# A planned attention and GELU kernel: all engines' order found anew, pair 0's values in one transfer per four heads, the last output tile in two halves

## The chip, the cores and the metric

The kernel runs on one core of a Trainium2 chip. The metric is device microseconds (us) of one execution. Before the change the median of three runs is 739.65 us (738.93 to 741.37).

## The reference, cut to what matters

Batch 8, 8 heads, 576 rows of 64 in q, k and v, and 32 packed queries p per head; then a feed-forward layer from 512 through 2048 to 512 on 4608 tokens. Everything is float32.

```python
def sm_attn(qq, kk, vv):
    s = scale * np.matmul(qq, kk.transpose(0, 1, 3, 2))
    s = s - np.max(s, axis=-1, keepdims=True)
    a = np.exp(s)
    a = a / (np.sum(a, axis=-1, keepdims=True) + 1e-09)
    return np.matmul(a, vv)
p_packed = sm_attn(p, k, v)          # 32 packed rows per head
out = sm_attn(q, p_packed, p_packed)
x = out.transpose(0, 2, 1, 3).reshape(4608, 512)
h = x @ w_in                         # 512 -> 2048
g = 0.5 * h * (1.0 + erf(h * inv_sqrt2))
return g @ w_out                     # 2048 -> 512
```

## The kernel before, in words

**What is computed where.** The eight batches form four pairs. Heads are taken in chunks of four: chunk 1_0 in a name is batch 1, first four heads. For a chunk TensorE (PE) turns k and q by transposes (`turn`, L461: tiles km, qm, copied to kT, qT on ScalarE (ACT) or VectorE (DVE)), multiplies the packed queries with kT (s1, L538), and DVE and ACT make the first softmax of it. Its exponentials are turned (e1Tm, e1Tn, L650) and multiplied with the values v (tile pp, L680), turned back (ppTm, L695) and copied to the SBUF tile pp. The second scores (s2, L538) are qT times pp; their softmax, on DVE and ACT with one chunk of pair 0 partly on GpSimd (POOL), gives the weights a2 (plain) and a2T (a pair of rounded parts, L804 and L806).

Instead of attention times w_in, the kernel multiplies pp with w_in first (wps, L1017, copied to wp) and then wp with the weights (h, L1083; L1074 for batch 0's first column block, where the plain weights serve). GELU follows on ACT (graw, L1106), its result is split into a rounded part and a rest (g, L1113 on ACT and L1115 on DVE), and these go against w_out (o, L1136 to L1138, three products for float32). Sums over column blocks lie in acc (L1200).

**Units and steps.** d_ff is cut into 4 blocks of 512 columns; a unit is one pair with one block, so 16 units of 8 steps (2 batches by 4 column tiles of 128), 128 steps in all. Step n has a hidden product h_n and output products o. The rows that a batch of 576 leaves over from tiles of 128 are gathered in t4 and multiplied after each unit (o_edge); the last of these ends the program. Units 0 to 3 also decode w_in and w_out (`decode`, L946 and L942 load, then ACT, DVE and POOL) and store them in DRAM (`keep`, L998) for the later units.

**What sets the order.** Nothing is ordered by hand. While the program is built, a small planner (`Order`, with `Op` for each piece of work) plays the engines through with costs that stand in the code, and the order in which it issues pieces becomes each engine's fixed instruction order. Of the ready pieces it takes the one with the lowest step number. The tables FIRST (pair 0 and unit 0), SECOND (pair 1) and LATER (pairs 2, 3) hold these step numbers; LEAD, PATIENCE and STEADY move weights and set how far a fitting piece may be taken ahead. A transfer's planned length comes from its cost: number of pieces and bytes over DMA_RATE, where the byte count is a fitted one, not the real one.

All transfers are issued by SyncE (SP) in one queue in planned order. A buffer that is not free stops this queue: of x raw tiles (k and q) there are 3, of raw values 1 (chunk 0_1 uses a buffer of wp instead), of raw weights 3.

Until the first output product, the planner fills PE's free time with products of a constant tile (`keep_warm`, L1056, tile still). They stand in PE's instruction order like others.

**Lines that the change touches.** `load` (k and q), `load_values` (v; pair 0 uses `sixths`, 96 partitions with six rows of each of four heads, in two pieces of 256 and 128 values per head and partition), `held`, `weight` and `decode`, `edge_output`, and the tables.

Of the kernel before, what the change touches and what calls it, by code (L numbers as in the profile page):

```python
# [42 lines left out]
DMA_FIRST, DMA_ISSUE, DMA_START, DMA_END, DMA_RATE = 2.0, 0.5, 0.6, 0.9, 390e3  # L43

DMA_DEPTH = 8
DMA_SLACK, DMA_EARLY = 2.0, 50.0
TABLE_SWITCH = 1.3
PE_START, PE_WINDOW, PE_LEAST = 1.0, 3.41, {True: 0.45, False: 0.9}
IDLE, IDLE_END = 0.11, 150.0
# [2 lines left out]


LATER = {
    "p": (11.96, 4.31),
    "k": (9.37, 6.72, -0.79, 5.76),
    "v": (4.46, 5.97, 10.35, 23.09),
    "q": (7.94, 14.96, 23.74, 28.45),
    "scores1": (-2.56, 15.38),
    "softmax1": (8.43, -1.96, 4.16, 5.99),  # L60
    "packed": (-50.68, -7.0, 15.26, 19.97),
    "scores2": (22.79, 15.93),
    "softmax2": (-77.33, -62.89, 23.22, 15.85),
    "weights2": (32.15, -50.98, -6.98, 38.51),
    "groups1": ((0, 1, 2, 3),),
    "groups2": ((0, 1), (2, 3)),
}

SECOND = {
    "p": (20.75, 3.34),  # L70
    "k": (7.37, -42.06, 10.92, 22.21),
    "v": (8.64, 9.54, 12.08, 14.62),
    "q": (24.0, -36.23, 19.77, 24.5),
    "scores1": (-7.96, 8.69),
    "softmax1": (23.58, 28.48, 10.35, 11.22),
    "packed": (13.43, 9.46, -19.64, 17.8),
    "scores2": (-42.32, 23.44),
    "softmax2": (3.08, -54.42, 7.07, 36.08),
    "weights2": (7.31, 23.91, -34.4, 27.85),
    "groups1": ((0,), (1,), (2,), (3,)),  # L80
    "groups2": ((0,), (1,), (2,), (3,)),
}

AHEAD = 12
LEAD = {"load": 41.5, "decode": -5.8, "packed_w_in": 12.3}

PATIENCE = {PE: -50.7, ACT: -58.2, DVE: 28.6, POOL: 30.2, DMA: -16.5}
STEADY = {PE: 50.0, ACT: -44.9, DVE: 8.1, POOL: -12.5, DMA: 13.9}

FIRST = {  # L90
    "p": (-317.54, -182.89),
    "k": (-327.51, -303.62, -196.02, -185.2),
    "v": (-249.99, -74.38, -178.71, -155.31),
    "q": (-216.51, -212.03, -93.83, -161.52),
    "w": (-194.95, -219.42, -192.91, -163.65, -152.43, -145.84, -71.43, -169.98),
    "scores1": (-221.37, -193.05, -72.18, -73.16),
    "softmax1": (-51.37, 6.81, -347.66, -175.1),
    "packed": (-180.43, -262.75, -182.09, 5.22),
    "scores2": (-233.03, -212.25, -155.17, -251.0),
    "softmax2": (-146.14, -327.21, -189.22, -190.15),  # L100
    "weights2": (-183.99, -138.74, -180.16, -74.68),
    "decode": (-178.03, -74.98, -180.05, -168.82, -193.1, -214.82, -193.35, 17.95),
    "packed_w_in": (-192.13, -218.39, -190.45, -146.14),
    "weights_split": (-94.13, -184.63, -65.79, -335.34),
    "groups1": ((0, 1), (2, 3)),
    "groups2": ((0,), (1,), (2,), (3,)),
    "gpsimd": (0,),
    "copy": ("ACT", "DVE", "DVE", "DVE"),
    "banks": (False, True, True, True),
    "turn": {"k": ("ACT", "DVE", "ACT", "ACT"), "q": ("ACT", "DVE", "ACT", "ACT")},  # L110
}


# [39 lines left out]
class Op:  # L153
# [1 line left out]


    def __init__(self, engine, cost, step, fn, takes=(), table=None, busy=True, port=False, tiled=False):
        self.engine, self.cost, self.step, self.fn = engine, cost, step, fn
        self.takes, self.table, self.busy, self.tiled = takes, table, busy, tiled

        self.port = (engine == POOL and cost > 0) or port


class Order:
# [147 lines left out]
def packed_attention_gelu_ffn(ctx: ExitStack, tc: tile.TileContext, q, k, v, p, w_in, w_out, out):  # L312
# [108 lines left out]
    def load(bt, name, src, c, step):  # L421

        def rows(t):
            nc.sync.dma_start(t, src[bt.b, 4 * c:4 * c + 4].rearrange("h (x s) d -> (h x) (s d)", s=2 * NT))

        def blocks(t):

            t = t.rearrange("p (n a) -> p n a", a=32)
            for hh in range(2):
                h0 = 4 * hh + 2 * c  # L430
                view = src[bt.b, h0:h0 + 2].rearrange("g (c b) (j a) -> j b (g c) a", b=32, j=2)
                for j in range(2):
                    i = 2 * hh + j
                    nc.sync.dma_start(t[32 * i:32 * i + 32], view[j])

        cost, fn = ((1, 570e3), rows) if bt.b < 2 else ((4, 1800e3, 1.1), blocks)
        bt.raw[name, c] = yield Op(DMA, cost, step, fn, [(xraws, f"{name}_{bt.n}_{c}")])
        fire(bt.loaded[name, c])

# [34 lines left out]
    def sixths_of(t):  # L474

        if len(t.shape) > 2:
            t = t.rearrange("p a b c -> p (a b c)").bitcast(F32)
        return t[:96, 0:24 * D].rearrange("p (g t d) -> p g t d", g=4, t=6)

    def load_values(s, step):  # L480
        heads = slice(4 * s.hh, 4 * s.hh + 4)

        def sixths(t):
            src = v[s.b, heads].rearrange("g (p t) d -> p g t d", t=6)
            for part in (slice(0, 4), slice(4, 6)):
                nc.sync.dma_start(
                    sixths_of(t)[:, :, part].rearrange("p g t d -> p g (t d)"),
                    src[:, :, part].rearrange("p g t d -> p g (t d)"))

        def fn(t):  # L490
            main, tail = values_of(t)
            nc.sync.dma_start(
                main.rearrange("p g t d -> p g (t d)"), v[s.b, heads, 0:512].rearrange("g (p t) d -> p g (t d)", t=4))
            nc.sync.dma_start(tail, v[s.b, heads, 512:S].rearrange("g p d -> p g d"))

        cost, fn = ((2, 700e3), sixths) if s.b < 2 else ((2, 900e3, 0.6), fn)
        s.v = yield Op(DMA, cost, step, fn, [(s.v_ring, f"v_{s.n}")])
        fire(s.v_loaded)

# [315 lines left out]
    reached = [Event() for _ in range(NU * 8)]  # L815

    def held(task, step):
        if step >= 1:
            yield reached[min(int(step), NU * 8 - 1)]
        yield from task  # L820
# [90 lines left out]
    def weight(u, i, load_steps, steps):  # L911


        ring_, home, k = (wis, wi, i) if i < 2 else (wos, wo, i - 2)
        n, f = f"{u}_{i}", u % NF
        if u >= NF:
            yield stored[f, i]
            home[u, k] = yield Op(
                DMA, (1, 524e3), steps[0],
                lambda t: nc.sync.dma_start(t.bitcast(F32), scratch[f, i]), [(ring_, f"w_{n}")])  # L920
            for part in range(parts_of(i)):
                fire(w_ready[u, i, part])
            return
        yield [decode(u, i, part, *at) for part, at in enumerate(zip(load_steps, steps))]
        d = scratch[f, i] = dram.tile([P, 2, FB], F32, name=f"ws_{f}_{i}")
        start(keep(f, i, d, home[u, k], steps[-1] + 4))

    def decode(u, i, part, load_step, step):
        n, f = f"{u}_{i}_{part}", u % NF
# [15 lines left out]
            src = w_in[2 * P * i:2 * P * i + 2 * P, c0:c0 + FB // 2].rearrange("(g p) n -> p g n", g=2)  # L945
            nc.sync.dma_start(t.rearrange("p (g n) -> p g n", g=2), src.bitcast(I32))  # L946

        raw = yield Op(DMA, (1, 540e3 if i < 2 else 500e3), load_step, fetch, [(raws, f"wraw_{n}")])
        low, high = words(raw)[:, :, 0], words(raw)[:, :, 1]

        def both_words(both):
# [14 lines left out]
            port=True)  # L966
        raws.give(raw)
        if i < 2:
            if (u, i) not in wi:
                got = yield from one(wis, f"w_{u}_{i}", POOL, step)  # L970
                wi[u, i] = got
            d, cols = wi[u, i], slice(part * (FB // 2), (part + 1) * (FB // 2))

            def halves(x):
                return x.rearrange("p (g n) -> p g n", g=2)

            yield Op(
                POOL, 1.25, step,
                lambda: nc.gpsimd.tensor_tensor(d[:, :, cols].bitcast(I32), halves(t), halves(full), ALU.add))  # L979
        else:  # L980
            def split():
# [306 lines left out]
```

## Time and profile before

| | us |
|---|---|
| median of 3 runs | 739.65 |
| profiled execution | 740.66 |
| its span (first to last instruction) | 738.9 |
| PE busy | 728.0 |
| DVE busy | 399.6 |
| ACT busy | 357.4 |
| POOL busy | 149.5 |

The profiled execution is 1.8 us longer than its span and 1.0 us above the median. PE busy counts the products of the constant tile too. Times in the trace are from the span's start. In the trace, a product that fills a PSUM tile first used by constant products carries that tile's name, so "PE idle L680" is a packed-values product; only "idle L1056" is the constant tile.

### The profile page before, as it was taken

To read this page: it belongs to the slowest core of one execution; us is meant where nothing else is said; L and a number is where in the kernel's file an instruction comes from. 1 tells how busy PE (TensorE), PEld (TensorE's weight loads), DVE (VectorE), ACT (ScalarE), POOL (GpSimd) and SP (SyncE) were. 2 spreads that over 40 slices of the span, in tenths; PEclk is the share of its full clock that TensorE was granted. 3 is DMA by queue.
4 is the path that set the end of the run, shared out by engine and by line. 5 is a ranking of instruction groups with operands and counts; after the bars stand their busy time and mean duration, and the time that the engine had idled before them with its cause. 6 is when DMAs were issued, how large, how long until landed. Compare 5 with 4: busy or idle time off the path is not lost.

```text
span 738.9 us, 13425 instructions
## 1 busy us (share of the span) xinstructions
PE 728.0 (99%) x5395; PEld 592.4 (80%) x5395; DVE 399.6 (54%) x604; ACT 357.4 (48%) x600; POOL 149.5 (20%) x328
## 2 busy tenths in 40 slices
PE   7999999999999999999999999999999999999998
PEld 5767888787877888788787888787877888888886
DVE  2779687888778432533756632553565821333332
ACT  2668674666766543454434444453443643323221
POOL 1334564654401101001100101100011110111010
PEclk8999999999999999999999999999999999999999
DMA  9967597667965697441734959263345703021022
GB/s 269 320 211 150 181 244 209 209 201 193 244 169 107 209 124 182 62 147 61 148 97 136 273 77 166 65 147 109 82 126 118 243 14 123 37 82 61 5 94 88
DMA packets 156589, 106.77 MB, mean 145 GB/s; under 512 B 123248, under 2 KB 132464, under 8 KB 156528
## 3 DMA queue, kind: packets, MB, share of 16 engines
q1 hardware_dynamic: 156528, 105.93, 55.3%
q8 instruction: 42, 0.69, 0.4%
q14 instruction: 19, 0.16, 0.1%
HBM read 83.89 MB, written 22.02 MB: 143 GB/s over the span
## 4 chain that ended last, share of the span: by engine, by line
PE 95%; DMA 3%; SPq 1%; issue 1%; DVE 0%; ACT 0%
PE h L1083 26%; PE o L1136 17%; PE o L1138 16%; PE o L1137 16%; PE wps L1017 4%; PE s L538 2%; PE o_edge L1136 2%; PE o_edge L1138 2%; PE o_edge L1137 2%; PE idle L1056 2%; DMA k<-in_k_dram 2%; DMA wraw<-in_moe_w_out_dram 2%; PE pp L680 2%; PE e1Tm L639 1%; PE h L1074 1%
## 5 line engine op out<-in xcount | busy, mean ns | idle before, releaser
L1083 PEld LDWEIGHTS h<-a2T,wp 128*128 128x128 f32 x1488 | 209.6, 188 | 11.4 <-ACT graw L1106 1.0
L1083 PE MATMUL h<-a2T,wp 128*128 128x288 f32 x1488 | 216.4, 294 | 0.8 <-ACT graw L1106 0.8
L1115 DVE TENSOR_TENSOR g<-graw,g 128x512 fp32r<-128x512 f32 x128 | 93.7, 734 | 212.4 <-ACT g L1113 212.2
L1106 ACT ACTIVATE graw<-h 128x576 f32<-128x576 f32 x127 | 82.8, 652 | 257.2 <-PE h L1083 197.0
L1136 PE MATMUL o<-w,g 128*128 128x512 f32 x508 | 205.7, 405 | 0.0
L1138 PE MATMUL o<-w,g 128*128 128x512 f32 x508 | 199.2, 392 | 0.0
L1137 PE MATMUL o<-w,g 128*128 128x512 f32 x508 | 198.8, 391 | 0.0
L1126 POOL CAST t<-graw 128x64 fp32r<-128x64 f32 x128 | 35.6, 278 | 504.1 <-ACT graw L1106 343.2
L1136 PEld LDWEIGHTS o<-w,g 128*128 128x128 f32 x508 | 95.3, 188 | 38.3 <-issue 22.5
L1138 PEld LDWEIGHTS o<-w,g 128*128 128x128 f32 x508 | 95.3, 188 | 21.9
L1137 PEld LDWEIGHTS o<-w,g 128*128 128x128 f32 x508 | 95.5, 188 | 14.8
L1200 DVE TENSOR_TENSOR acc<-o,acc 128x512 f32<-128x512 f32 x96 | 64.0, 686 | 41.6 <-PE o L1138 41.5
L1113 ACT CAST g<-graw 128x512 fp32r<-128x512 f32 x128 | 79.3, 620 | 9.9 <-PE o L1138 6.9
L1127 POOL TENSOR_TENSOR t<-graw,t 128x64 fp32r<-128x64 f32 x128 | 45.6, 356 | 10.2
L1033 DVE TENSOR_TENSOR wp<-wps,wp 128x1024 fp32r<-128x1024 f32 (+1 forms) x32 | 37.7, 1186 | 18.0 <-ACT wp L1028 17.9
L1028 ACT CAST wp<-wps 128x1024 fp32r<-128x1024 f32 x30 | 30.1, 1014 | 22.4 <-PE wps L1017 22.4
L1017 PE MATMUL wps<-w,pp 64*32 64x512 f32 (+1 forms) x544 | 34.4, 574 | 0.0
L1056 PE MATMUL idle<-still 128*128 128x256 bf16 x231 | 31.8, 288 | 1.1 <-DVE still L394 1.1
L1056 PEld LDWEIGHTS <-still 128*128 128x128 bf16 x231 | 22.8, 102 | 9.1 <-issue 4.5
L952 ACT ACTIVATE wt<-wraw 128x512 f32<-128x512 f32 x32 | 21.6, 676 | 16.3 <-POOL w L993 7.5
L979 POOL TENSOR_TENSOR w<-wt 128x512 int32<-128x512 int32 x16 | 22.0, 1373 | 28.2 <-DVE mx L610 15.9
L960 DVE TENSOR_SCALAR wt<-wt 128x512 int32<-128x512 int32 x32 | 25.4, 792 | 1.1
(127 smaller groups left out, 663.4 us busy)
## 6 DMA issues: line engine op xcount, KB each, us to landing
w<-ws SPq DMA_DIRECT2D x72, 512.0 KB, 4.9
ws<-w SPq DMA_DIRECT2D x24, 512.0 KB, 4.8
wraw<-in_moe_w_in_dram SPq DMA_DIRECT2D x16, 512.0 KB, 5.3
wraw<-in_moe_w_out_dram SPq DMA_DIRECT2D x16, 512.0 KB, 3.6
k<-in_k_dram SPq DMA_DIRECT2D x48, 144.0 KB, 4.7
q<-in_q_dram SPq DMA_DIRECT2D x48, 144.0 KB, 4.8
out_dram<-acc SPq DMA_DIRECT2D x27, 256.0 KB, 2.3
v<-in_v_dram SPq DMA_DIRECT2D x12, 512.0 KB, 5.6
```

The lines of the kernel that those rows point to most:

```text
L1017: nc.tensor.matmul(t[r0:r0 + 32, hh, :m], lhsT=pp[b][rows, hh, r0:r0 + 32], rhs=wi[u, hh][rows, g, cols], start=True, stop=True)
L1033: yield Op(DVE, 0.16 + 1.04 * m / FB, step, lambda: nc.vector.tensor_tensor(lo, x, hi.bitcast(F32), ALU.subtract))
L1056: nc.tensor.matmul(bank(t)[:, :256], lhsT=still[:, :P], rhs=still, start=True, stop=True)
L1083: nc.tensor.matmul(t[:, half, :HALF], lhsT=w[:, wpart, ch, fc], rhs=a2T[b, ch][:, apart, half * HALF:(half + 1) * HALF], start=ch == 0 and ...
L1106: lambda raw: nc.scalar.activation(raw.rearrange("p (a n) -> p a n", a=2), t[:, :, :HALF], AF.Gelu),
L1113: g = yield Op(ACT, 0.52, lead, lambda g: nc.scalar.copy(g[:, 0], main), [(gts, f"g_{n}")])
L1115: DVE, 0.6, lead, lambda: nc.vector.tensor_tensor(g[:, 1], main, g[:, 0].bitcast(F32), ALU.subtract),
L1127: nc.gpsimd.tensor_tensor(dst[:, 1], side, dst[:, 0].bitcast(F32), ALU.subtract)
L1136: nc.tensor.matmul(t, lhsT=g[0], rhs=w[:, 0], start=first, stop=False)
L1137: nc.tensor.matmul(t, lhsT=g[0], rhs=w[:, 1], start=False, stop=False)
L1138: nc.tensor.matmul(t, lhsT=g[1], rhs=w[:, 0], start=False, stop=last)
L1200: yield Op(DVE, 0.6, n, lambda: nc.vector.tensor_tensor(a, x, a, ALU.add))
```

## The change

Four things change.

1. The numbers in FIRST, SECOND, LATER, LEAD, PATIENCE and STEADY, with a new table `keep` for the stores of decoded weights. Chunk 0_1 takes GpSimd's part instead of chunk 0_0.
2. The planner's lengths of the first transfers: k and q of pair 0 from 570e3 to 620e3 bytes, w_in from 540e3 to 590e3, w_out from 500e3 to 530e3, values of pair 0 from two pieces of 700e3 together to one of 1000e3; the 2 us that it adds to a landing now start at 6 us instead of 50 us.
3. The values of pair 0 come in one transfer per chunk, with 384 values per head and partition.
4. The last o_edge (unit 15) is made in two halves of 256 columns, each with its own addition and store.

```diff
-DMA_SLACK, DMA_EARLY = 2.0, 50.0
+DMA_SLACK, DMA_EARLY = 2.0, 6.0
...
-    "v": (-249.99, -74.38, -178.71, -155.31),
...
+    "v": (-334.59, -165.81, -182.85, -96.68),
...
-        cost, fn = ((1, 570e3), rows) if bt.b < 2 else ((4, 1800e3, 1.1), blocks)
+        cost, fn = ((1, 620e3), rows) if bt.b < 2 else ((4, 1800e3, 1.1), blocks)
...
         def sixths(t):
-            src = v[s.b, heads].rearrange("g (p t) d -> p g t d", t=6)
-            for part in (slice(0, 4), slice(4, 6)):
-                nc.sync.dma_start(
-                    sixths_of(t)[:, :, part].rearrange("p g t d -> p g (t d)"),
-                    src[:, :, part].rearrange("p g t d -> p g (t d)"))
+            nc.sync.dma_start(
+                sixths_of(t).rearrange("p g t d -> p g (t d)"), v[s.b, heads].rearrange("g (p t) d -> p g (t d)", t=6))
...
-        cost, fn = ((2, 700e3), sixths) if s.b < 2 else ((2, 900e3, 0.6), fn)
+        cost, fn = ((1, 1000e3), sixths) if s.b < 2 else ((2, 900e3, 0.6), fn)
...
-        raw = yield Op(DMA, (1, 540e3 if i < 2 else 500e3), load_step, fetch, [(raws, f"wraw_{n}")])
+        raw = yield Op(DMA, (1, 590e3 if i < 2 else 530e3), load_step, fetch, [(raws, f"wraw_{n}")])
...
+        if u == NU - 1:
+            yield from last_output(u, n)
+            return
...
+    def last_output(u, n):
+        a, r0, m = acc[NP - 1, 4], (NP - 1) * 2 * S + 4 * P, DM // 2
+        def add(t, cols):
+            yield Op(DVE, 0.36, n, lambda: nc.vector.tensor_tensor(a[:, cols], t[:, 0, :m], a[:, cols], ALU.add))
+            yield Op(DMA, (1, 131e3), n, lambda: nc.sync.dma_start(out[r0:r0 + P, cols], a[:, cols]))
+        for k in range(2):
+            cols = slice(k * m, k * m + m)
+            def product(t, cols=cols):
+                for c in range(NC4):
+                    g = t4[u, c]
+                    three(t[:, 0, :m], (g[:, 0], g[:, 1]), wo[u, c][:, :, cols], c == 0, c == NC4 - 1)
+            t = yield Op(PE, 1.38, n, product, [(wide, f"o_{u}_edge_{k}")])
+            start(add(t, cols))
```

How the instructions move shows at three places. The names end in running numbers; the numbers before them are batch and chunk (v_0_1 is chunk 0_1) or, for w and wraw, unit, tile and part (tiles 0 and 1 are w_in, 2 to 5 w_out).

SP's queue, its first two dozen rows. Before:

```order
L424 DMA k_0_1_93<-in_k_dram 128x1152
L486 DMA v_0_0_97<-in_v_dram 96x4x256
L486 DMA v_0_0_97<-in_v_dram 96x4x128
L946 DMA wraw_0_0_1_104<-in_moe_w_in_dram 128x2x512
L424 DMA q_0_0_109<-in_q_dram 128x1152
...
L424 DMA k_1_1_257<-in_k_dram 128x1152
L486 DMA v_0_1_275<-in_v_dram 96x4x256
L486 DMA v_0_1_275<-in_v_dram 96x4x128
L998 DMA ws_0_0_318<-w_0_0_78 128x1024
...
L424 DMA q_1_0_416<-in_q_dram 128x1152
L998 DMA ws_0_1_415<-w_0_1_79 128x1024
L486 DMA v_1_0_554<-in_v_dram 96x4x256
```

The same stretch with the change:

```order
L425 DMA k_0_0_97<-in_k_dram 128x1152
L485 DMA v_0_0_101<-in_v_dram 96x4x384
L425 DMA q_0_0_105<-in_q_dram 128x1152
...
L485 DMA v_0_1_123<-in_v_dram 96x4x384
...
L425 DMA k_1_1_281<-in_k_dram 128x1152
L941 DMA wraw_0_5_0_316<-in_moe_w_out_dram 128x1024
L997 DMA ws_0_0_379<-w_0_0_78 128x1024
L485 DMA v_1_0_419<-in_v_dram 96x4x384
L941 DMA wraw_0_4_0_430<-in_moe_w_out_dram 128x1024
...
L425 DMA q_1_0_559<-in_q_dram 128x1152
```

Values of chunk 0_1 stood behind all of k and are now the ninth row; values of chunk 1_0 stood behind all of q and now stand ahead of batch 1's q.

PE, around the packed values of batch 0. Before:

```order
L461 MATMUL km_1_1_2_425<-ident_71,k_1_1_257 128x128 x3
L538 MATMUL idle_349<-kT_1_0_357,pT_1_307 32x288 x8
L680 MATMUL pp_0_1_440<-v_0_1_275,e1T_0_1_309 32x64 x24
...
L538 MATMUL s1_1_1_493<-kT_1_1_405,pT_1_307 32x288 x8
...
L680 MATMUL idle_505<-v_0_0_97,e1T_0_0_474 32x64 x24
L538 MATMUL s2_0_1_0_544<-qT_0_1_333,pp_0_502 32x288 x4
...
L1017 MATMUL wps_0_0_1_601<-w_0_0_78,pp_0_502 32x256 x2
```

With the change:

```order
L678 MATMUL idle_310<-v_0_1_123,e1T_0_1_229 32x64 x24
...
L678 MATMUL idle_367<-v_0_0_101,e1T_0_0_354 32x64 x24
...
L508 MATMUL pTm_1_432<-ident_71,p_1_147 128x128 x2
L693 MATMUL ppTm_0_1_435<-ident_71,pn_0_1_416 128x128
...
L693 MATMUL idle_439<-ident_71,pn_0_0_437 128x128
...
L1016 MATMUL idle_259<-w_0_0_78,pp_0_446 32x256 x2
...
L536 MATMUL s2_0_0_0_479<-qT_0_0_238,pp_0_446 32x288 x4
...
L462 MATMUL km_1_0_0_490<-ident_71,k_1_0_232 128x128 x3
```

Batch 0's packed values, its first wps and its first second scores stood behind batch 1's k and its first scores; now they stand ahead of them.

PE, the first output products. Before:

```order
L1017 MATMUL wps_0_1_1_879<-w_0_0_78,pp_1_734 32x256 x2
...
L1074 MATMUL h_2_977<-a2_0_716,wp_0_0_84 128x288 x4
L1136 MATMUL idle_868<-w_0_2_537,g_0_891 128x512
...
L1074 MATMUL h_3_1022<-a2_0_716,wp_0_0_84 128x288 x4
L1083 MATMUL h_4_1035<-a2T_1_0_971,wp_0_1_478 128x288 x6
L1083 MATMUL h_4_1035<-a2T_1_1_1020,wp_0_1_478 128x288 x6
```

With the change:

```order
L1073 MATMUL h_2_908<-a2_0_746,wp_0_0_84 128x288 x4
L536 MATMUL s2_1_1_929<-qT_1_1_705,pp_1_736 32x288 x8
L1135 MATMUL idle_893<-w_0_2_426,g_0_913 128x512
...
L1016 MATMUL wps_0_1_1_953<-w_0_0_78,pp_1_736 32x256 x2
...
L1073 MATMUL h_3_983<-a2_0_746,wp_0_0_84 128x288 x4
...
L1016 MATMUL wps_0_1_0_1022<-w_0_0_78,pp_1_736 32x256 x2
...
L1082 MATMUL h_4_1060<-a2T_1_0_920,wp_0_1_361 128x288 x6
L1082 MATMUL h_4_1060<-a2T_1_1_1044,wp_0_1_361 128x288 x6
```

Two wps products of batch 1 moved behind the first output product, and the outputs of steps 0 to 2, not of step 0 alone, now stand ahead of h_4. Ahead of the first output product PE's order has 231 constant products before and 208 with the change; otherwise the same pieces but for those two wps.

## Rows read from the trace of the kernel before

**Rows 1.** The page: busy time and share of PE; its granted clock by slices.

```profile
PE 728.0 (99%) x5395; PEld 592.4 (80%) x5395; DVE 399.6 (54%) x604; ACT 357.4 (48%) x600; POOL 149.5 (20%) x328
...
PEclk8999999999999999999999999999999999999999
```

**Rows 2.** Waits of PE: engine, line, releaser: us in total, times, longest.

```profile
PE km L461 <- DMA k<-in_k_dram: 3.1, 1, 3.1
PE idle L461 <- DMA k<-in_k_dram: 1.2, 1, 1.2
...
PE idle L680 <- issue: 1.0, 1, 1.0
PE h L1083 <- ACT graw L1106: 0.8, 1, 0.8
```

**Rows 3.** The chain that ended last, 31 to 70 us: start, length, what.

```profile
36.61 0.69 PE idle L680 x40
...
39.95 1.75 PE idle L1056 x16
41.70 1.02 PE wps L1017 x32
...
43.48 0.65 PE s L538 x16
...
45.14 0.66 PE qm L461 x6
45.79 0.81 PE pp L680 x48
...
64.77 1.94 PE h L1074 x8
66.72 0.23 PE idle L1136
```

**Rows 4.** The chain that ended last, 730 to 739 us: its last row.

```profile
735.24 0.69 DVE acc L1200
```

**Rows 5.** Timeline of PE: the first constant products (start, length, line, operation, count).

```profile
1.05 3.59 PE L1056 MATMUL idle<-still 128*128 128x256 bf16 x16 [1.05 <-DVE still L394]
```

**Rows 6.** Windows of the start: busy us per engine, granted clock, DMA share, GB/s.

```profile
0.00:5.00 5.00, 3.90 (x18) 2.58 (x19) 0.17 (x1) 1.49 (x2) 0.70 (x6) 1.00 0.62 167
...
8.60:15.40 6.80, 6.00 (x49) 3.25 (x49) 3.29 (x6) 1.23 (x2) 0.00 (x0) 0.50 1.08 310
...
25.00:29.00 4.00, 3.99 (x37) 3.50 (x36) 3.58 (x6) 0.96 (x2) 1.57 (x2) 1.00 1.10 258
...
34.00:38.00 4.00, 3.30 (x73) 2.23 (x72) 1.59 (x3) 2.42 (x6) 2.07 (x3) 1.00 0.28 113
5.00:12.00 7.00, 3.92 (x34) 3.09 (x34) 1.95 (x4) 1.34 (x3) 0.00 (x0) 0.76 1.06 227
12.00:25.00 13.00, 13.00 (x125) 9.74 (x110) 7.30 (x19) 8.21 (x17) 2.56 (x2) 0.87 1.04 394
38.00:67.00 29.00, 28.67 (x396) 21.50 (x397) 25.39 (x47) 21.51 (x41) 11.87 (x15) 1.00 0.81 203
```

**Rows 7.** SP's timeline of issues: start, length, line, what.

```profile
21.86 0.85 SPq L486 DMA_DIRECT2D v<-in_v_dram  x2
...
38.71 0.85 SPq L486 DMA_DIRECT2D v<-in_v_dram  x2
```

**Rows 8.** Timeline of DVE: a copy of 256 columns; first and last operation of chunk 1_1's weights.

```profile
22.92 0.42 DVE L516 COPY pT<-idle 128x256 f32<-128x256 f32 x1 [1.55 <-PE idle L510]
...
56.61 0.48 DVE L729 STREAM_TRANSPOSE e<-idle 128x288 f32<-128x288 f32 x1 [0.23 <-PE s L538]
...
69.03 0.76 DVE L806 TENSOR_TENSOR a2T<-a,a2T 128x576 fp32r<-128x576 f32 x1 [0.96 <-ACT a2T L804]
```

**Rows 9.** The page, part 6: issues of output stores, KB each, us to landing.

```profile
out_dram<-acc SPq DMA_DIRECT2D x27, 256.0 KB, 2.3
...
out_dram<-acc SPq DMA_DIRECT2D x36, 64.0 KB, 1.7
```

More of the change, by code (lines that the diff above doesn't have):

```diff
@@ L54 @@
 LATER = {
[L55 to L64, printed above, removed]
+    "p": (4.57, 0.36),
+    "k": (9.77, 1.03, 7.85, 4.86),
+    "v": (-19.28, 1.49, 8.02, 25.08),
+    "q": (10.43, 8.08, 12.34, 27.12),
+    "scores1": (-8.06, 24.15),
+    "softmax1": (12.29, 4.77, 15.35, 60.41),
+    "packed": (-150.33, -17.64, 0.7, 19.71),
+    "scores2": (62.5, -1.6),
+    "softmax2": (-150.15, 24.03, -1.71, 11.31),
+    "weights2": (-8.65, -21.33, 4.8, 19.35),
     "groups1": ((0, 1, 2, 3),),
@@ L69 @@
 SECOND = {
[L70 to L80, printed above, removed]
+    "p": (-20.93, -4.93),
+    "k": (-28.97, 4.94, 9.77, -51.85),
+    "v": (-61.37, -55.81, -54.58, 5.26),
+    "q": (12.48, 7.19, 17.01, 14.56),
+    "scores1": (16.49, 10.44),
+    "softmax1": (70.49, 59.26, -0.03, -5.23),
+    "packed": (-65.26, -12.66, 14.32, 29.2),
+    "scores2": (0.83, -443.94),
+    "softmax2": (-441.05, 63.77, 63.42, -66.47),
+    "weights2": (28.35, -35.63, -442.25, 9.65),
+    "groups1": ((0, 1, 2, 3),),
     "groups2": ((0,), (1,), (2,), (3,)),
@@ L84 @@
 AHEAD = 12
-LEAD = {"load": 41.5, "decode": -5.8, "packed_w_in": 12.3}
-PATIENCE = {PE: -50.7, ACT: -58.2, DVE: 28.6, POOL: 30.2, DMA: -16.5}
-STEADY = {PE: 50.0, ACT: -44.9, DVE: 8.1, POOL: -12.5, DMA: 13.9}
+LEAD = {"load": -11.11, "decode": 1.13, "packed_w_in": 252.72, "keep": 8.35}
+PATIENCE = {PE: -146.2, ACT: -31.9, DVE: 92.3, POOL: 107.3, DMA: 81.9}
+STEADY = {PE: 78.2, ACT: -28.4, DVE: -17.4, POOL: -12.9, DMA: -55.7}
 FIRST = {
-    "p": (-317.54, -182.89),
-    "k": (-327.51, -303.62, -196.02, -185.2),
-    "v": (-249.99, -74.38, -178.71, -155.31),
[L94 to L105, printed above, removed]
@@ new lines @@
+    "p": (-449.28, -149.82),
+    "k": (-368.84, -450.82, -157.17, -141.84),
+    "v": (-334.59, -165.81, -182.85, -96.68),
+    "q": (-326.21, -264.65, -68.55, -136.32),
+    "w": (-309.63, -184.59, -388.91, -135.47, -158.04, -132.41, -19.99, -64.57),
+    "scores1": (-460.85, -139.3, -466.68, -127.88),
+    "softmax1": (-34.71, -168.91, -154.78, -325.2),
+    "packed": (-150.12, 59.54, -386.64, -105.4),
+    "scores2": (-138.79, -178.59, -173.06, -336.05),
+    "softmax2": (-163.88, -135.68, -346.68, -179.95),
@@ L106 @@
+    "weights2": (-31.57, -153.15, -109.93, -150.61),
+    "decode": (-128.55, -350.82, -35.75, -69.29, -154.8, -427.3, -127.97, -183.87),
+    "packed_w_in": (-318.66, -439.74, 58.95, -191.69),
+    "weights_split": (-128.83, -345.1, -184.29, -142.96),
+    "keep": (28.54, -184.99, -157.74, -161.76, -128.25, 61.28),
+    "groups1": ((0,), (1,), (2,), (3,)),
     "groups2": ((0,), (1,), (2,), (3,)),
-    "gpsimd": (0,),
-    "copy": ("ACT", "DVE", "DVE", "DVE"),
-    "banks": (False, True, True, True),
@@ L110 @@
-    "turn": {"k": ("ACT", "DVE", "ACT", "ACT"), "q": ("ACT", "DVE", "ACT", "ACT")},
+    "gpsimd": (1,),
+    "copy": ("DVE", "ACT", "ACT", "ACT"),
+    "banks": (True, True, True, False),
+    "turn": {"k": ("ACT", "DVE", "ACT", "DVE"), "q": ("DVE", "ACT", "ACT", "ACT")},
 }
@@ L157, in __init__ @@
     def __init__(self, engine, cost, step, fn, takes=(), table=None, busy=True, port=False, tiled=False):
-        self.engine, self.cost, self.step, self.fn = engine, cost, step, fn
+        self.engine, self.cost, self.step, self.fn = engine, cost, round(step, 3), fn
         self.takes, self.table, self.busy, self.tiled = takes, table, busy, tiled
@@ L817, in held @@
     def held(task, step):
+        step = round(step, 3)
         if step >= 1:
@@ L925, in weight @@
         d = scratch[f, i] = dram.tile([P, 2, FB], F32, name=f"ws_{f}_{i}")
-        start(keep(f, i, d, home[u, k], steps[-1] + 4))
+        start(keep(f, i, d, home[u, k], steps[-1] + (FIRST["keep"][i] if u == 0 else LEAD["keep"])))
     def decode(u, i, part, load_step, step):
@@ L968, in decode @@
         if i < 2:
-            if (u, i) not in wi:
+            if u > 0:
                 got = yield from one(wis, f"w_{u}_{i}", POOL, step)
```

## The prediction

> **What bounds the kernel now.** I read the page first: PE is busy 728.0 of 738.9 us and its clock is full in all slices but the first [rows 1]. So only PE time can be won, and the waits say where: 3.1, 1.2 and 1.0 us early on, and one of 0.8 us in all the rest [rows 2]. The reader is to see that after the third of these, at 38 us, PE is never idle again but for those 0.8 us. Yet it isn't all work: 231 constant products stand in PE's order ahead of the first output product. In the chain that product starts at 66.72 us [rows 3], and from there PE does 668.5 us of gapless work up to 735.2 us [rows 4]. The change is worth what it moves this start by, less the work that it moves behind it, plus what it saves at the end.
>
> How much of the 66.7 us is work? By pieces of the order and their lengths in the chain [rows 3]: 80 transposes of 128 by 0.11 us (6 in 0.66) are 8.8, 24 narrower ones at the same length 2.6, 8 score products by 0.65 are 5.2, 4 packed-values products by 0.81 are 3.2, 4 wps by 0.51 are 2.0, 3 h of 1.94 are 5.8. That is 27.6 us. The 231 constant products by 0.109 (16 in 1.75) are 25.2. Together 52.8 us; the other 13.9 us are the start at 1.05, the three waits (5.3), 1.8 us because the first 16 constant products took 3.59 instead of 1.75 us [rows 5], some 3 us because the granted clock was 0.50, so the 1.2 GHz level, from 8.6 to 15.4 us [rows 6], and about 2.5 us that I can't place.
>
> **The order found anew.** The same sum for the changed order has 23 constant products fewer (2.5 us) and two wps fewer (1.0): 49.3 us. With the start and the slow first 16 this is 52.2 us, the earliest that the first output product can start. With all 13.9 us of before it is 63.2. The two ends are far apart, so I walk two paths to it.
>
> Path one is the loads. In the changed queue q_1_0 is the last load that batch 1 needs except one set of values. Up to it there are 8 tiles of k and q and 3 of values of 0.59 MB, 8 raw weights and 3 stores of 0.52, and 0.26 of p: 12.5 MB. 0.8 MB are moved in the first 5 us, and 394 GB/s is the rate where no values are under way [rows 6]: 11.7 MB take 29.7 us, to 34.7. Values are slow: while they moved, 227 GB/s were reached over 7 us and 258 over 4 us [rows 6], which lost (394-227)/394 x 7 = 3.0 and (394-258)/394 x 4 = 1.4 us. Three of them now stand ahead of q_1_0: 4.2 to 9.0 us, so it lands at 38.9 to 43.7. The queue's last transfers come in at a thin 113 GB/s [rows 6], which may add up to 3 us; I take 42. Behind q_1_0's landing PE's order has 3 groups of transposes (1.0), 10 constant products (1.1), two narrow groups (0.7), a score product (0.65), 10 constant (1.1), h_0 (1.94), 2 constant (0.2), pp (0.8), h_1 (1.94), a transpose and 8 constant (1.0), h_2 (1.94) and a score product (0.65): 13.0 us. First output at 52 to 59 us, 55 in the middle.
>
> Path two is PE's own queue. k_0_0 is now behind one weight tile: 5 us + 1.1 MB at 394 GB/s is 7.8 us, or 10.8 if the values behind it cost it the 3.0 us. From its transposes to the first output the changed order holds 44.7 of the 49.3 us: 52.5 to 55.5, and 58.9 if a wait there brings the 1.2 GHz clock for as long as before (3.4 us). The later of two paths of about 55 counts, and before had one small wait of 1.0 us besides: I take **57.0 us**.
>
> Why so much sooner than 66.7? Before, chunk 0_0's packed values were multiplied at 36.6 us [rows 3], behind batch 1's k and s1, because chunk 0_1's values were issued only at 21.86 us, and chunk 1_0's values had to wait for that buffer until 38.71 us [rows 7], when no load was under way any more. Now pp of batch 0 needs only loads up to the ninth row (4.7 MB, by the same rates some 16 to 21 us), and batch 0's softmax runs beside batch 1's loads.
>
> **What the start hides.** ACT, DVE and POOL get the same operations in another order. DVE is busy 25.4 of 29 us between 38 and 67 us [rows 6], so it could become late. From s2 of chunk 1_1 to its last operation took 13.2 us before (56.6 to 69.8) [rows 8]; the changed PE order covers it by three steps' outputs of 2.76 us, h_3 and two wps, 11.2 us, and h_4's first half (0.8). If it again takes 13.2 us PE waits 1.2 us at h_4; DVE's new order has 15 operations there, and by some 0.6 us each, between the 0.48 and the 0.76 of those rows, that is 9 us, so I take 0.
>
> **Values in one piece.** It saves one issue of some 0.42 us on SP per chunk (two took 0.85 [rows 7]), hidden while loads queue up. Whether the rate changes no row shows: nothing gained, or all the loss of 1.4 to 3.0 us per chunk. I take nothing, since in the trace both pieces lie in the same slow stretches. [...] The other way path one would be 4 to 9 us shorter, and path two alone would give about 55.5 us.
>
> **The last tile in halves.** The first half's addition and store lie beside the second half's products. The addition behind the last product falls from 0.69 us [rows 4] to about the 0.42 of a 256-column copy [rows 8], and the store's 2.3 us for 256 KB lie between that and 1.7 for 64 KB [rows 9], so 128 KB saves 0.1 to 0.4: together 0.4 us. PE streams the same columns: 256 take 0.109 as a constant product and 0.115 as half of the 0.23 for 512 [rows 3], so 24 of them cost between 0.1 us less and nothing; I take nothing.
>
> **Later pairs.** Their order changes too, but PE waited 0.8 us once in 670 us and has the same products. I take 0; up to 1 us either way.
>
> **The sum.** 57.0 + 668.5 + 1.0 (the two wps) = 726.5 us to the last product; the end took 738.9 - 735.2 = 3.7 and now 3.3: a span of 729.8 us. The profiled execution was 1.8 us above its span and 1.0 above the median, so the median comes to **730.5 us**, 9.1 us less than 739.65.
>
> **The rivals.**
> 1. *The waits only move.* If PE loses the same 13.9 us besides its order's sum, the first output starts at 63.2 and the time is 736.7 us. For it: new loads (k_0_0, v_0_1, q_1_0) stand just ahead of their products, and PE can't pass a late one; an early wait brought the 1.2 GHz clock for 6.8 us [rows 2, 6]. Against it: the waits of 1.2 and 1.0 us were followed by no such stretch, and the planner now counts the first transfers as longer. Chance 0.22 for 733.5 to 737.4. The Trainium skill says in "TensorE: Matmul & The Clock Gate", section "What's actually happening", that half rate is TensorE's default, to which idle time returns it. The trace agrees for the wait of 3.1 us; each further such stretch would cost some 3 us again.
> 2. *Values are slower still, and the time is longer.* Three are now ahead of q_1_0. The gain is gone when the first output starts at 66.1, so q_1_0 lands at 53: 11 us, or 3.7 per chunk, beyond the 2.2 assumed. A chunk then takes 1.5 + 2.2 + 3.7 = 7.4 us, 80 GB/s. At 60 GB/s (9.8 us each) the first output would start at 73.3 and the time be 746.8 us. Against it: both slow stretches moved 227 and more in all. Chance 0.05.
> 3. *The start is given back.* DVE must have its share done in 9 us less; at 88% [rows 6] that is 7.9 us of work left behind at the first output product. If PE has to wait for all of it in the next steps, the time is 738.4 us, and 737.4 to 740 with some of the waits. The same would be seen if the new order did nothing of what its plan says. Against it: DVE is at 54% over all [rows 1], and before, at that 88%, PE didn't wait for it. Chance 0.10.
>
> **How the numbers follow.** The forecast, 727 to 733.5 us (first output at 53.5 to 60), has 0.60; better than 727, near the earliest possible start, 0.03. The range 727 to 737 us takes in most of rival 1 and leaves out 0.18. About 0.3%, 2.2 us, can be told from no change, so up to 737.4 is faster: 0.60 + 0.03 + 0.22 = 0.85; within 0.10; slower 0.05.
>
> **What would show it.** Right: the first output product at 53 to 60 us, no load in the row of waits for over 2 us, values of chunk 1_0 issued at 22 to 29 instead of 38.71 us, PE gapless from the first output product on, 3.3 us from the last product to the end. Wrong: a wait for q_1_0 or k of more than 3 us, a second long stretch at clock 0.50, or waits of PE for DVE or ACT after 57 us of more than 2 us in all.

## The result, and the profile after

The changed kernel takes 731.47 us (median of 4 runs, 730.74 to 735.64); the kernel before, beside it, takes 739.83 us (4 runs, 738.93 to 741.37). The ratio is 0.9897, interval 0.9856 to 0.9937: 8.4 us faster. Run again on chips 14 and 9, the changed kernel gave 732.18 us (0.9907, 0.9889 to 0.9925) and 731.09 us (0.9890, 0.9875 to 0.9904). The forecast was 730.5 us, range 727 to 737.

The page of the profiled execution (731.66 us, span 729.9) has PE busy 5.0 us less than in [rows 1], and its clock is full in the first slice too:

```profile
PE 723.0 (99%) x5384; PEld 589.8 (81%) x5384; DVE 400.2 (55%) x605; ACT 353.6 (48%) x597; POOL 149.1 (20%) x328
...
PEclk9999999999999999999999999999999999999999
```

The waits of PE (engine, line, what it waited for: us in total, times, longest). This is the whole list; against [rows 2] a wait for k is left, those for GELU and at the packed values are gone:

```profile
PE idle L462 <- DMA k<-in_k_dram: 2.5, 2, 2.4
PE idle L1055 <- DVE still L395: 1.1, 1, 1.1
```

The chain that ended last (start, length, what), from its first transfer on and at its end:

```profile
2.67 7.97 DMA k<-in_k_dram
10.68 0.55 PE idle L462 x3
...
726.49 0.13 PE o_edge L1137
726.62 0.02 issue
726.64 0.42 DVE acc L1192
```

The first rows say what the start is now: k_0_0 is issued at 2.67 us and lands at 10.64, its transposes begin at once, and from there the chain stays on PE to 726.62. The addition at the end is 0.42 us instead of 0.69 [rows 4].

The first output product, in PE's timeline (start, length, line, operation); by the same view it started at 66.34 before:

```profile
57.05 0.50 PE L1135 MATMUL idle<-w,g 128*128 128x512 f32 x1
```

Windows (busy us of each engine with instructions, granted clock, DMA share, GB/s), to be laid beside [rows 6]. PE has no gap from 12 to 726 us. In the last row it does 669 us of products with DVE busy little more than half of the time. The rate in 5 to 12 us is 298 GB/s with a set of values under way, and 410 and 414 later:

```profile
0.00:5.00 5.00, 3.77 (x17) 2.45 (x18) 0.17 (x1) 1.49 (x2) 0.71 (x6) 1.00 0.61 166
5.00:12.00 7.00, 4.61 (x48) 3.67 (x48) 4.19 (x9) 1.97 (x4) 1.27 (x1) 1.00 1.06 298
12.00:25.00 13.00, 13.00 (x210) 11.02 (x208) 9.45 (x19) 8.56 (x20) 2.72 (x3) 1.00 1.05 327
25.00:29.00 4.00, 4.00 (x68) 2.79 (x57) 3.77 (x5) 2.57 (x8) 3.41 (x5) 1.00 1.03 410
34.00:38.00 4.00, 4.00 (x49) 3.17 (x47) 3.86 (x11) 2.92 (x6) 2.38 (x2) 1.00 1.03 414
38.00:57.00 19.00, 19.00 (x248) 14.93 (x240) 16.91 (x31) 15.22 (x32) 9.23 (x12) 1.00 0.97 295
57.00:726.00 669.00, 669.00 (x4701) 548.15 (x4694) 357.02 (x522) 316.58 (x522) 127.68 (x299) 1.00 0.54 133
```

SP's issues of the values of pair 0 (start, length): chunks 0_0, 0_1, 1_0, 1_1, the last two at 25.23 and 41.27 us. Chunk 0_1's was issued at 21.86 and 1_0's at 38.71 before [rows 7].

```profile
3.18 0.43 SPq L485 DMA_DIRECT2D v<-in_v_dram  x1
5.52 0.47 SPq L485 DMA_DIRECT2D v<-in_v_dram  x1
25.23 0.33 SPq L485 DMA_DIRECT2D v<-in_v_dram  x1
41.27 0.33 SPq L485 DMA_DIRECT2D v<-in_v_dram  x1
```

So the gain is where it was forecast: the first output product starts 9.3 us earlier, and the whole span is 9.0 us shorter. The tables were changed as a whole, so which of the moved pieces makes the gain no run parts; that it is the values' earlier issues, as the prediction has it, is argued from these rows and not shown.

### The profile page after: what moved, and what is told of

Same layout as the page of the kernel before. It is cut to its first block, busy times and chain, and to the rows that moved or that the text cites. A ratio compares the mean times of both kernels' runs of the same rounds, so it can differ in the third digit from the quotient of the medians.

```text
span 729.9 us, 13392 instructions
## 1 busy us (share of the span) xinstructions
PE 723.0 (99%) x5384; PEld 589.8 (81%) x5384; DVE 400.2 (55%) x605; ACT 353.6 (48%) x597; POOL 149.1 (20%) x328
## 4 chain that ended last, share of the span: by engine, by line
PE 98%; DMA 1%; SPq 0%; DVE 0%; issue 0%
PE h L1082 27%; PE o L1135 17%; PE o L1137 16%; PE o L1136 16%; PE wps L1016 4%; PE idle L1055 3%; PE s L536 2%; PE o_edge L1135 2%; PE o_edge L1137 2%; PE o_edge L1136 2%; PE pp L678 1%; DMA k<-in_k_dram 1%; PE h L1073 1%; PE e1Tm L637 1%; PE qm L462 1%; PE idle L678 0%
## 5 line engine op out<-in xcount | busy, mean ns | idle before, releaser
L1114 DVE TENSOR_TENSOR g<-graw,g 128x512 fp32r<-128x512 f32 x128 | 95.5, 748 | 214.2 <-ACT g L1112 210.8
L1126 POOL TENSOR_TENSOR t<-graw,t 128x64 fp32r<-128x64 f32 x128 | 45.3, 354 | 10.3
L1027 ACT CAST wp<-wps 128x1024 fp32r<-128x1024 f32 (+1 forms) x32 | 31.2, 986 | 15.0 <-PE wps L1016 15.0
L1055 PE MATMUL idle<-still 128*128 128x256 bf16 x208 | 27.9, 284 | 1.1 <-DVE still L395 1.1
L986 POOL TENSOR_TENSOR wt<-wt 128x512 int32<-128x512 int32 x16 | 22.9, 1430 | 22.5 <-DVE wt L964 20.5
L1135 PE MATMUL o_edge<-w,t 128*128 128x512 f32 (+1 forms) x68 | 25.9, 382 | 0.0
```

Of the source, the lines that this page charges most:

```text
L1055: nc.tensor.matmul(bank(t)[:, :256], lhsT=still[:, :P], rhs=still, start=True, stop=True)
L1114: DVE, 0.6, lead, lambda: nc.vector.tensor_tensor(g[:, 1], main, g[:, 0].bitcast(F32), ALU.subtract),
L1126: nc.gpsimd.tensor_tensor(dst[:, 1], side, dst[:, 0].bitcast(F32), ALU.subtract)
L1135: nc.tensor.matmul(t, lhsT=g[0], rhs=w[:, 0], start=first, stop=False)
```

## The experiments

**Order or one piece?** The kernel before, with its order, takes its values in one piece.

```diff
-            src = v[s.b, heads].rearrange("g (p t) d -> p g t d", t=6)
-            for part in (slice(0, 4), slice(4, 6)):
-                nc.sync.dma_start(
...
+            nc.sync.dma_start(
+                sixths_of(t).rearrange("p g t d -> p g (t d)"), v[s.b, heads].rearrange("g (p t) d -> p g (t d)", t=6))
```

> The kernel before, every engine's order kept, with pair 0's values in one piece. Theory A (the order makes the gain): PE's own order of 231 constant products stays, only the waits for k (3.1 and 1.2 us) can shrink by up to 1 us each: first output product at 65 to 66.7 us, span 737 to 739. Theory B (values in one piece make much of the gain): first output product at 60 to 64 us, span 732.5 to 736.

Measured: 738.41 us, ratio 1.0004 (0.9992 to 1.0016), first output product at 65.01 us. That is theory A: in the old order the one piece gives nothing that can be measured (the interval is 0.9 us either way), so the rest of the change makes the gain.

**The lengths behind the tables.** After, with the planner's old lengths (and the old DMA_EARLY) under the new tables.

```diff
-DMA_SLACK, DMA_EARLY = 2.0, 6.0
+DMA_SLACK, DMA_EARLY = 2.0, 50.0
...
-        cost, fn = ((1, 620e3), rows) if bt.b < 2 else ((4, 1800e3, 1.1), blocks)
+        cost, fn = ((1, 570e3), rows) if bt.b < 2 else ((4, 1800e3, 1.1), blocks)
...
-        cost, fn = ((1, 1000e3), sixths) if s.b < 2 else ((2, 900e3, 0.6), fn)
+        cost, fn = ((2, 700e3), sixths) if s.b < 2 else ((2, 900e3, 0.6), fn)
...
-        raw = yield Op(DMA, (1, 590e3 if i < 2 else 530e3), load_step, fetch, [(raws, f"wraw_{n}")])
+        raw = yield Op(DMA, (1, 540e3 if i < 2 else 500e3), load_step, fetch, [(raws, f"wraw_{n}")])
```

> The changed kernel with the new tables of step numbers, but the planner's old lengths of the first transfers. Its PE order has 304 constant products ahead of the first output product instead of 208, with the same work. Theory (a constant product is not waited for by anyone but PE itself, so PE's queue sets the start): 96 more by 0.109 are 10.5 us; first output product at 65 to 68 us, span 738 to 741. Rival (loads and the other engines set the start, constant products only fill): first output at 57 to 60 us, span 730 to 733.

Measured: 751.25 us, ratio 1.0183 (1.0153 to 1.0213). The order that comes out has 304 constant products ahead of the first output product, 96 more than after (10.5 us at 0.109), and PE waits for ACT and DMA at more places, some of them late, in pair 1. Three of its eleven rows of waits:

```profile
PE idle L462 <- DMA k<-in_k_dram: 2.7, 1, 2.7
PE ppTm L693 <- ACT pn L686: 1.3, 1, 1.3
...
PE idle L462 <- DMA q<-in_q_dram: 1.0, 1, 1.0
```

The first output product starts at 73.02 us, 63.2 us behind the landing of k_0_0 (9.86), where after has 46.4. The direction was right, the size too small: of the 16.8 us more, 10.5 are the constant products, 3.6 are six waits behind that landing, and about 1.2 are two wps that this order has ahead of the first output product, so the work ahead of it was not the same as expected. Behind it come 2.8 us of waits in pair 1. The new tables without the lengths under which they were found are worse than the kernel before; the old tables under the new lengths were not measured.

**One piece or two in the new order.** After, with the loop of two pieces (1024 and 512 bytes per head and partition) put back; all engines but SP keep their order.

> The changed kernel, every engine's order kept, with pair 0's values in two pieces of 256 and 128 values again. Theory A (values go at their slow rate in one piece or two, the gain is the order's): first output product at 57 to 58 us, span 729.5 to 731. Theory B (the single piece made the values faster, and that let the new order work): each of the first three loads of values ends 1 to 2 us later, q_1_0 lands at 44.5 to 47 instead of 41.5 us, the first output product starts at 58.5 to 61 and the span is 731.5 to 734 us.

Measured: 733.21 us, ratio 0.9931 (0.9913 to 0.9949), 1.7 us more than after's median. In the profile q_1_0 lands at 44.55 us (41.54 after), the first output product starts at 60.14, and PE waits for values:

```profile
PE idle L462 <- DMA k<-in_k_dram: 3.2, 1, 3.2
PE idle L681 <- DMA v<-in_v_dram: 1.4, 2, 1.2
```

That is theory B, some 3 us in the load path for three chunks. But k_0_0, which stands ahead of all values, landed at 11.66 us too, 1.0 later than after, and the weight tile ahead of it at 8.44 (7.54 after), so much of the delay need not come from the pieces. So two more kernels went to it. The first has the same bytes in two transfers of whole runs, cut by heads:

```diff
-            nc.sync.dma_start(
-                sixths_of(t).rearrange("p g t d -> p g (t d)"), v[s.b, heads].rearrange("g (p t) d -> p g (t d)", t=6))
+            src = v[s.b, heads].rearrange("g (p t) d -> p g (t d)", t=6)
+            for part in (slice(0, 2), slice(2, 4)):
+                nc.sync.dma_start(
+                    sixths_of(t)[:, part].rearrange("p g t d -> p g (t d)"), src[:, part])
```

> After, but each chunk's values of pair 0 come in two transfers by heads (two heads each, whole runs of 384 values, 1536 bytes), on the same 96 partitions; all engines' orders are unchanged. It parts two readings of the run in which the two pieces were cut by rows (1024 and 512 bytes) and cost about 1 us per chunk. Theory A, the length of the contiguous runs is what costs: the two transfers by heads are as fast as the one, the second of chunk 0_1 lands at 20 to 21.5 us, q_1_0 at 41 to 42.5, the first output product at 57 to 58, median 730.5 to 732.5. Theory B, it is the second transfer as such: chunk 0_1 is complete at 22.5 to 24 us, q_1_0 lands at 43.5 to 45, the first output product at 59 to 60.5, median 732.5 to 734.

Measured: 731.97 us (4 runs, 730.38 to 735.31), ratio 0.9901 (0.9868 to 0.9934). It parts nothing: the median is theory A's, the profiled execution (first output product at 59.04, chunk 0_1 complete at 22.71) theory B's, with k_0_0 at 10.88 and a stretch at clock 0.50. Its two executions at a mean clock of 0.999 and 1.00 took 730.48 and 730.38 us, the two at 0.997 and 0.998 took 733.46 and 735.31. The second is the kernel with two pieces again, and beside it, on the same chip, the changed kernel itself.

> After with the values of pair 0 in two pieces by rows again (1024 and 512 bytes), on one chip beside the changed kernel itself. Theory A, the one piece is worth the 1.8 us that the two medians showed, or more: this kernel is 1.5 to 3 us slower than after beside it, v_0_1 is complete at 22.5 to 24 us and q_1_0 lands at 43.5 to 45. Theory B, that difference lay between executions and not between kernels: the two are within 1 us of each other, and the loads land within 1 us of those of after beside it.

> The changed kernel itself, on one chip beside the one with two pieces. Both theories: 731 to 732.5 us, 0.989 to 0.991 of before, v_0_1 at 20 to 21 us, q_1_0 at 41 to 42, first output product at 57 to 58. Theory A has the kernel with two pieces 1.5 to 3 us above it, theory B within 1 us.

Measured: two pieces 731.46 us (730.76 to 732.66), ratio 0.9892 (0.9877 to 0.9908); one piece 731.09 us (730.11 to 733.33), ratio 0.9890 (0.9875 to 0.9904). Theory B of this pair holds: the two are within 1 us of each other. In the execution with two pieces v_0_1 is complete 10.2 us behind k_0_0, with one piece 9.7, and q_1_0 lands 30.8 us behind k_0_0 in both. So the 1.7 us between the first run and after were not the two pieces' as such. The first run's own chip says the same: the kernel with the whole last tile, which takes its values in one piece, had 733.42 us there, and two pieces 733.21. Open is the load path alone: v_0_1 is complete 12.2 and 11.8 us behind k_0_0 in the first two profiles with two transfers, and 9.7 to 11.0 in six with one. Chain and timeline of this run of the changed kernel:

```profile
2.67 6.42 DMA k<-in_k_dram
9.13 0.55 PE idle L462 x3
```

```profile
55.50 0.50 PE L1135 MATMUL idle<-w,g 128*128 128x512 f32 x1
```

And the first output product of the kernel with two pieces beside it, with k_0_0 at 9.61 us:

```profile
56.08 0.50 PE L1138 MATMUL idle<-w,g 128*128 128x512 f32 x1
```

From the landing of k_0_0 to the first output product it is 46.41 us here (9.09 to 55.50), 46.47 with two pieces (9.61 to 56.08) and 46.41 in the first profile of after (10.64 to 57.05). **The start of this kernel is the landing of k_0_0 plus 46.4 us**, with one piece or two, as long as nothing is waited for behind that landing and the clock stays at 1.00.

**The last tile in halves.** After, without them.

```diff
-        if u == NU - 1:
-            yield from last_output(u, n)
-            return
```

> The changed kernel with its last output tile whole again. Theory: the halves are worth 0.3 to 0.5 us, all of it behind the last product: last product at the same 726.6 us, then 3.6 to 3.7 us to the end of the span instead of 3.3; span 730.2 to 730.4. Rival: the halves cost PE as much as they save at the end (24 products of 0.12 us against 12 of 0.23): span 729.9 as with them.

Measured: 733.42 us, ratio 0.9928 (0.9906 to 0.9951). Most of that is again the start (k_0_0 at 11.32, first output product at 59.32). The end can be read by itself in the chain:

```profile
728.52 0.24 PE o_edge L1137
728.76 0.02 issue
728.78 0.69 DVE acc L1218
```

From the end of the last product to the end of the span it is 3.78 us here (728.75 to 732.53) and 3.28 after (726.60 to 729.88). From the first output product to the end of the last one it is 669.43 and 669.55 us. The halves save 0.5 us at the end and cost PE 0.1: about 0.4 us, as the theory has it, though the last product did not end at the same time (728.75 and not 726.6 us).

**The wait for k_0_0.** 22 more constant products ahead of its transposes; beside it the changed kernel.

```diff
         def product(m):
+            if name == "km_0_0_0":
+                for _ in range(22):
+                    nc.tensor.matmul(m[:, :256], lhsT=still[:, :P], rhs=still, start=True, stop=True)
             for n in range(3):
```

> The changed kernel with 22 more constant products (2.4 us) in PE's order just ahead of k_0_0's first transposes, where it waits 2.4 us. Theory (the wait costs its own length and, in some runs, a stretch at the 1.2 GHz clock after it): no wait for k over 1 us and no stretch at 0.50 before 40 us; the time of an undisturbed run doesn't change, first output at 57 to 58 us, and the runs lie closer together, highest within 2 us of the lowest, median 730.5 to 732. Rival (the clock after the wait doesn't matter): same median and spread as the changed kernel beside it.

> The changed kernel as it is, beside the runs below on one chip. First output product at 57 to 58 us where the clock stays at 1.00 after the wait for k_0_0, at 59 to 60 where a stretch at 0.50 follows; median 731 to 733.5 us.

Measured: 732.67 us with the cover (6 runs, 731.4 to 735.68), ratio 0.9916 (0.9896 to 0.9937); 732.18 us without (731.37 to 733.73). The wait is gone and the clock is 1.00 throughout in the profile:

```profile
8.12 2.51 PE idle L462 x22
```

The cover ran to 10.63 us, and k_0_0 had landed at 9.65, so it held the transposes up for a microsecond; the first output product starts 47.1 us behind that landing, 0.7 more than 46.4. The spread is not narrower, and runs of 733.5 us with a mean clock of 1.00 are among them. So the clock behind this wait is not all that spreads the runs of this kernel. In the changed kernel itself the clock does part them: of its 15 executions on record, the ten with a mean clock of 0.999 or 1.00 took 730.11 to 732.05 us, the five with 0.995 to 0.998 took 732.31 to 735.64. In the profile of after beside it the window behind the wait is

```profile
10.84:14.24 3.40, 3.40 (x30) 1.80 (x27) 0.32 (x2) 1.46 (x4) 0.07 (x1) 0.50 1.02 339
```

and the first output product starts 48.0 us behind k_0_0 (9.71 to 57.72), 1.6 us more than 46.4. 48.0 and 48.2 us are also what the whole tile and the two transfers by heads show, which have such a stretch too.

**A load moved.** Chunk 0_0's values one row later in SP's queue, behind q_0_0.

```diff
-    "v": (-334.59, -165.81, -182.85, -96.68),
+    "v": (-320.0, -165.81, -182.85, -96.68),
```

> The changed kernel with the values of chunk 0_0 one row later in SP's queue, behind q_0_0; all other rows and engines in the same order. Theory (values slow the transfer just ahead of them): k_0_0 lands at 8.3 to 9.3 instead of 10.6 us, its wait falls from 2.4 to under 1 us, the first output product starts at 55.5 to 56.5 us, span 728 to 729.5. Rival (k_0_0 is late because of what is ahead of it): it lands at 10.3 or later, first output at 57 to 58 us, span 729.5 to 731.

Measured: 732.06 us, ratio 0.9902 (0.9885 to 0.992). k_0_0 lands at 9.62, but PE now waits for the values of chunk 0_1, and the first output product starts at 57.91:

```profile
PE idle L678 <- DMA v<-in_v_dram: 1.8, 1, 1.8
PE idle L1055 <- DVE still L395: 1.1, 1, 1.1
PE idle L462 <- DMA k<-in_k_dram: 0.9, 1, 0.9
```

The theory missed, and the rival's 10.3 us too: k_0_0 landed at 9.71 in the changed kernel beside it, so here its landing did not hang on the values behind it. Nothing is gained, since the values of chunk 0_1 are the next load that is just in time (after, they land at 20.46 and are used from 20.75). The first output product starts 48.3 us behind k_0_0, which is 46.4 and the wait of 1.8.

**Fewer constant products.** After, with every second constant product behind the first 16 left out (96 fewer, 10.5 us of PE's queue).

```diff
                 t = r.next("idle")
-                nc.tensor.matmul(bank(t)[:, :256], lhsT=still[:, :P], rhs=still, start=True, stop=True)
+                constant[0] += 1
+                if constant[0] <= 16 or constant[0] % 2:
+                    nc.tensor.matmul(bank(t)[:, :256], lhsT=still[:, :P], rhs=still, start=True, stop=True)
```

> The changed kernel with every second constant product after the first 16 left out (96 of 208), all else in the same order. Theory (two paths of nearly one length, PE's own queue and the loads behind it): PE's queue is 10.5 us shorter, but q_1_0 lands 2.1 us ahead of its product and the values of chunk 1_1 1.3 us, so PE waits for loads instead; first output product at 54.5 to 56.5 us, span 727.5 to 729.5. Rival 1 (PE's queue alone sets the start): 47 to 50 us, span 720 to 723. Rival 2 (the constant products hold the clock): longer stretches at 0.50, first output at 58 to 62 us, span 731 to 735.

Measured: 731.22 us, ratio 0.9892 (0.9874 to 0.991); first output product at 56.95, no earlier than after. Most of the 10.5 us comes back as waits, 10.0 us in seven rows against 2.5 after (the first constant product's 1.1 us left out); these are the longest:

```profile
PE idle L678 <- DMA v<-in_v_dram: 4.8, 2, 3.6
PE idle L462 <- DMA k<-in_k_dram: 2.7, 1, 2.7
PE idle L462 <- DMA q<-in_q_dram: 1.1, 1, 1.1
```

A stretch at clock 0.50 from 23.13 to 26.54 us, behind the wait of 3.6 us, takes part of the rest. The last load that PE waits for is chunk 1_1's values:

```profile
41.00 9.80 DMA v<-in_v_dram
50.80 0.04 issue
50.84 0.88 PE idle L678 x48
```

After, these landed at 49.24 us and were used from 50.53. So the constant products of the new order lie almost wholly in time that the loads need anyway; the two paths are of nearly one length. To shorten the load path as well, the last kernel has half of the constant products and chunk 0_1's values issued ahead of two weight tiles:

```diff
-    "v": (-334.59, -165.81, -182.85, -96.68),
+    "v": (-334.59, -315.0, -182.85, -96.68),
```

> After, with every second constant product behind the first 16 left out (as in the run with half of them) and the values of chunk 0_1 issued ahead of two weight tiles instead of behind them; the planner then orders the other engines a little otherwise too. Theory A, in the run with half of the constant products the first load that was late set the start: its wait of 4.8 us for these values falls to 1 to 3 us, since 1.05 MB at 394 GB/s (2.7 us) fewer stand ahead of them, the first output product starts at 54 to 56 us, median 728.5 to 730.5. Theory B, all loads together set it, not this one: the wait goes on to a later load (q_1_0 at 42 us or later, batch 1's values), the first output product stays at 56.5 to 58.5, median 730.5 to 732.5.

Measured: 741.75 us, ratio 1.0034 (1.0012 to 1.0056); both theories miss. The values land at 19.10 us and their products start at 19.27, as theory A has it, but that one number changes the planner's order of the other engines too, and new waits come up, on other engines and behind the first output product (60.79 us) too:

```profile
PE km L462 <- DVE e L727: 3.7, 1, 3.7
...
PE wps L1016 <- POOL w L978: 2.4, 1, 2.4
...
PE s L536 <- ACT pp L697: 0.9, 1, 0.9
```

Three windows are at half clock, one of them at 77 us. It parts nothing about the load path. No version beat after by more than the runs spread.

## Why the prediction was right, point by point

- **What bounds the kernel: right.** PE has no gap from 10.68 us on, and the time moves with the first output product: 66.34 to 57.05 us, span 738.9 to 729.9. The 66.72 that I had read is the chain's: it lets an instruction begin where the one ahead of it ends (57.12 after).
- **The first output product: 57.0 forecast, 57.05 measured; the path was right, the agreement to 0.05 us is luck.** It came by a shorter sum and a spare microsecond, and three executions of the same kernel start at 55.50, 57.05 and 57.72. Path two is what set it. k_0_0 landed at 10.64 (I had 7.8 to 10.8). Behind it I had 44.7 us of order; measured are 46.4, with no wait in them. The missing 1.7 us are in the lengths of single rows: in the chain of the execution that started at 55.50, 183 constant products took 20.51 us (0.112 each; by my 0.109 19.9), 63 transposes 7.88 (0.125 each, since some groups of three took 0.48 and not 0.33; by my 0.11 6.9) and 2 wps 1.18 (by my 0.51 1.0). By the forecast's steps path two ended at 55.5 at the latest, and the microsecond that I set beside it for a small wait stood where these lengths belong. With it the sum is 56.5; the last 0.5 us of the 57.0 has no source in the prediction.
- **Path one: its size right, its last load wrong.** I had q_1_0 at 42 us; it landed at 41.54, 39.84 and 40.80 in three executions, and from its transposes (43.87) to the first output product it was 13.2 us, where I had 13.0. But it had 2.3 us to spare in the first. The load without slack is v_0_1, landing at 20.46 and used from 20.75: I gave it 16 to 21 us and then left it out of the paths:

```profile
20.75 0.88 PE L678 MATMUL idle<-v,e1T 96*32 96x64 f32 x48
```

The run with half of the constant products shows it binding, and chunk 1_1's values behind it, which path one set aside too: they had 1.3 us to spare after.
- **Values in one piece: nothing, right as far as about 1 us can be told.** The old order (1.0004) and the new one (731.46 and 731.09 us on one chip) agree. A single profile of each kernel had spoken for 3 us; side by side that fell: same partitions, other pieces, and landings behind k_0_0 within 0.5 us of each other in that pair.
- **No load wait over 2 us: wrong.** The wait for k_0_0 was 2.4 us, and 0.4 to 1.9 in the other two executions of the same kernel. In the forecast this was inside the range for k_0_0's landing, but the sign that I gave was too tight.
- **Values of 1_0 at 22 to 29 us:** 25.23. **The wait at h_4 for chunk 1_1's weights, taken at 0:** there is none.
- **Gapless from there on, later pairs 0:** 669.5 us forecast from the first output product to the last, 669.55 measured (669.50 in the chain's terms). That it fits so closely is luck again: the 668.5 us of before held the wait of 0.8 us for GELU, which is gone, and PE's work behind the first output product grew by 1.8 us where I had 1.0. Of that, two wps are 1.18 and the halves 0.1. Rival 3 (the start is given back) is out: DVE, busy 16.9 of 19 us ahead of the first output product, holds PE up nowhere.
- **The end:** 3.3 forecast and measured; halves 0.4 forecast and 0.4 measured, of which the addition is 0.27.
- **Rival 1 (the waits only move)** has happened in small. After it the wait for k_0_0 is followed in some executions by half a clock for 3.4 us; I had priced that at 3 us for a stretch of 6.8; it is half as long and costs 1.6, so the price by its length holds. In the time of the kernel before, that stretch was worth less than the 3 us of my sum, though: of its 50 executions beside these runs, the seven with a mean clock of 1.00 have a median of 738.69 us, the fifteen with 0.994 or 0.995 (as the profile with that stretch) 739.17.
- **The median:** 731.5 against 730.5. The profiled execution, 731.66, is 0.2 above its median, where I had carried over the 1.0 of before: that term, not the span (729.8 and 729.9), is the difference.

## What to carry to other kernels

Where the busy engine never waits after its first late load, that load's landing plus the queue behind it is the start, and a look for the second load without slack tells how much a shorter queue can give: here almost nothing. A difference of 2 us between two kernels whose own executions differ by 2 us is read only side by side on one chip, and best from a point that is common to both, here the landing of k_0_0, and among executions with the same mean clock. The interval of a ratio holds for its own set of runs: one kernel, with two pieces, gave 0.9931 (0.9913 to 0.9949) and 0.9892 (0.9877 to 0.9908) on two chips. A planner's table is a set of numbers for one set of costs: here one number changed (beside half of the constant products), and the costs alone, each cost more than the whole table brought.

## What the runs showed of the hardware that I had not expected

- With SP's first five issues the same, within 0.02 us, k_0_0 (issued at 2.66) landed at 9.09, 9.71 and 10.64 us in three executions of the changed kernel, and at 9.6 to 11.7 us in nine of its variants; the load ahead of it already differed (6.97 to 8.63 us). This goes into the time almost one to one where the clock is the same: 9.09 and 10.64 us gave spans of 728.3 and 729.9. Why transfers that are issued alike land 2.6 us apart, no run here shows.
- A wait of 1.9 us of PE was followed by 3.4 us at clock 0.50 in one execution, waits of 2.6 and 3.1 us in two others, and waits of 2.4 and 3.2 us were followed by none. Such a stretch cost 1.6 to 1.8 us of the start.
